# Background decoding of weights redistributed: six late pieces for twelve, w_sg between the halves of w_in, copies issued by ScalarE, later row stores

## The chip, the cores and the metric

The kernel runs on one core of one Trainium2 chip. The metric is the device time in microseconds (us), the median of three runs of the same program. Profiles come from one further execution, of which the hardware profiler recorded every instruction.

## The reference, cut to what matters

Three layers follow each other on a batch of 4 sequences of 576 rows; everything is float32 on entry to the matmuls, and the weights come as float64.

```
ret  = ((q @ k.T) / 8 * Dmat) @ v          # 8 heads of 64, Dmat = gamma_h ** (i - j) for i >= j, else 0
x    = ret, heads joined                   # 4 x 576 x 512
h    = gelu(x @ w_in);  u, v = h[:512], h[512:]
v_n  = (v - mean(v)) / sqrt(var(v) + 1e-6) * g_ln
v_s  = w_sg @ v_n + b_sg                   # w_sg is 576 x 576: it mixes rows of a sequence
x    = x + (u * v_s) @ w_out               # token mixer
xn   = (x - mean(x)) / sqrt(var(x) + 1e-6) * g_ln2
out  = x + relu(xn @ w_ch1) @ w_ch2        # channel mixer, 512 -> 2048 -> 512
```

## The kernel before

Every product is taken with float32 accuracy from three faster ones: an operand is split into a high part (`hi`, a rounded copy by ScalarE) and a low part (`lo`, the difference, by POOL or VectorE), and `mm3` multiplies hi with hi, hi with lo, lo with hi (lines 124 to 126).

**Stages, in order of time.** (1) The attention, 16 units (4 sequences by 4 pairs of heads), up to 82 us. A unit's inputs are one load `ld` (line 203; four buffers, issued three units ahead by SP, the queue of SyncE), prepared by ScalarE (`prep_unit`, line 218); its states are copied by ScalarE (`y`, line 252) and then decayed by VectorE (line 254). (2) The token mixer, batch by batch, 82 to 309 us: `v_tile` makes the five v tiles (`split_x`'s `xt_hi`, `xt_lo` by w_in's second half), whose rows are normalised (`bn_stats` at line 476 up to line 492) and split into `vnh`, `vnl`; `u_chunk` makes u; `sg_chunk` multiplies `vnh`, `vnl` by w_sg, adds b_sg (`b_bc`), multiplies u (lines 597, 600) and splits the result into `glh`, `gll` (lines 608 to 611); `w_out_tile` multiplies by w_out (line 661) and stores rows of x. In the batches' course `turn_x` transposes rows of the attention's result (line 632) and stores them to DRAM, from where they come back for the residual. The fifth v tile has 64 rows only; its rows are copied to the place where the next batch needs them by three DMAs (lines 550, 551). (3) The channel mixer, 309 us to the end: three blocks of rows by eight steps, 24 steps s in all; each step forms the products of one group of channel weights by seven products instead of eight, with VectorE instructions named `h`, `t`, `u` and `b` at lines 929 to 956, and 26 matmul triples with line 124 among them. The block's rows come as eight loads of features `x_raw` (line 764), scaled, combined by POOL (line 786) and split into `fe`.

**Background.** Weights are float64 in DRAM. A piece of 128 x 512 is loaded as words (`raw`, line 134, three buffers), decoded by four VectorE instructions (lines 142, 146, 149, 151) with one Square by ScalarE (line 148) before the last, and then either split into hi and lo (w_in, w_out) or stored back to DRAM as float32 (`w1_dram`, `w2_dram`, line 360, for the 32 pieces of the channel mixer). Decoded words `c` have two buffers. w_sg is float32: its five row groups (`raw_sg`, line 321, sharing the three `raw` buffers) are only split. All this is one generator, `background_steps`, and `background(n)` takes n steps of it; a step is one VectorE instruction of a piece, or one row group of w_sg. The calls stand in the code of the stages: twice one step a unit in the attention, and in the mixer after each v tile, u chunk, gate chunk and w_out tile as the table `PACE` says (a row per batch; the last row is for quarter steps of the channel mixer). `LATE` is the number of the 32 channel pieces that are left to the channel mixer. A new piece is loaded when one is taken up, so that one or two loads are ahead.

**Order.** The schedule is manual: every engine works through its instructions in the order in which the code issues them, SP's DMAs too. `after(n, f)` puts work off by n ticks; a tick follows each gelu and most other parts, and work that is due then is issued in turn, an instruction of each.

## Time and profile before

| | us |
|---|---|
| runs | 732.44, 731.85, 732.58; median 732.44 |
| profiled execution, device time | 730.41 |
| its span in the trace | 728.5 |
| attention | 0 to 82 |
| token mixer, batches 1 to 4 | 82 to 147.7, 206.0, 257.5, 309.2 |
| channel mixer, step 0, 1, 5, 7, 9, 15 begins | 309.2, 316.6, 401.8, 438.0, 474.3, 568.7 |

The span is the stretch between the first and the last instruction recorded; the device time has 1.9 us around it. TensorE's two clock levels here are 1.2 and 2.4 GHz, and a granted clock of 1.00 in a row means the higher one. The ends of the stages are the starts of the next stage's first matmul on TensorE; VectorE may still be at work for the stage before.

### The profile page before, as it was taken

The page shows a single profiled execution, that of the slowest core. Times are in us where ns is not written, and L with a number is a line of the kernel's source. Part 1 is how long each engine was busy: PE and PEld are TensorE (multiplying, and loading weights), DVE is VectorE, ACT ScalarE, POOL GpSimd, SP SyncE. Part 2 cuts the span into 40 slices and gives each one's busy share as a digit, 9 for nine tenths or more (in the row PEclk, how much of TensorE's full clock was granted, in tenths as well). Part 3 has the DMA queues.
Part 4 walks back from the last instruction along what each step waited for, and adds up shares of the span by engine and source line. Part 5 has one row for each costly group of instructions (what it writes and reads, how often), then busy time and mean ns, then how long its engine had stood idle before and what let it go on. Part 6 is the DMA issues. An engine that isn't in the chain of part 4 may idle for free.

```text
span 728.5 us, 11598 instructions
## 1 busy us (share of the span) xinstructions
PE 679.0 (93%) x4294; PEld 600.0 (82%) x4294; DVE 502.9 (69%) x929; ACT 289.3 (40%) x529; POOL 335.1 (46%) x302
## 2 busy tenths in 40 slices
PE   6989988899999998869878998999999899999997
PEld 4878887699899898667767787898988788989895
DVE  2889849799798879877887866566755655344333
ACT  2434445345346364423334444334434443333321
POOL 0321265725426435834443367555455845544511
PEclk9999998999999999889999999999999999999999
DMA  9998253485675694465574621453642144212132
GB/s 349 340 330 328 67 156 98 144 269 159 208 240 162 189 251 132 143 242 159 181 219 135 173 87 58 158 176 116 188 114 90 58 145 145 72 59 73 57 116 86
DMA packets 61960, 117.88 MB, mean 162 GB/s; under 512 B 6480, under 2 KB 25424, under 8 KB 59984
## 3 DMA queue, kind: packets, MB, share of 16 engines
q1 hardware_dynamic: 61904, 117.15, 50.5%
q8 instruction: 33, 0.54, 0.3%
q14 instruction: 23, 0.19, 0.1%
HBM read 89.07 MB, written 27.26 MB: 160 GB/s over the span
## 4 chain that ended last, share of the span: by engine, by line
PE 53%; DVE 17%; DMA 10%; POOL 7%; ACT 6%; issue 4%; SPq 2%; DVEq 0%; POOLq 0%; ACTq 0%
PE b L124 14%; PE b L126 14%; PE b L125 14%; PE b L661 7%; DMA ld<-in_attn_dram 4%; POOL mix L786 2%; DVE c L151 2%; DVE c L146 2%; DVE c L142 2%; SPq L764 1%; DVE h L929 1%; DMA raw_w<-w_dram 1%; DMA w_dram<-c 1%; PE o L285 1%; ACT h L928 1%
## 5 line engine op out<-in xcount | busy, mean ns | idle before, releaser
L124 PE MATMUL b<-fe,w 128*128 128x384 f32 x336 | 118.2, 352 | 22.4 <-DVE t L951 9.1
L729 POOL TENSOR_TENSOR w<-raw_w,w 128x512 fp32r<-128x512 f32 x46 | 61.9, 1346 | 127.3 <-ACT w L728 127.3
L125 PE MATMUL b<-fe,w 128*128 128x384 f32 x336 | 115.8, 345 | 0.0
L126 PE MATMUL b<-fe,w 128*128 128x384 f32 x336 | 115.8, 345 | 0.0
L126 PE MATMUL b<-w,h 128*128 128x512 f32 x288 | 114.7, 398 | 0.0
L124 PE MATMUL b<-w,h 128*128 128x512 f32 x288 | 114.5, 398 | 0.0
L125 PE MATMUL b<-w,h 128*128 128x512 f32 x288 | 114.2, 396 | 0.0
L928 ACT ACTIVATE h<-b 128x384 fp32r<-128x384 f32 x72 | 35.3, 491 | 151.0 <-DVE b L956 111.5
L124 PEld LDWEIGHTS b<-fe,w 128*128 128x128 f32 x336 | 64.7, 193 | 33.8 <-DVE t L951 12.6
L929 DVE SCALAR_TENSOR_TENSOR h<-b,h 128x384 fp32r<-128x384 f32 x72 | 40.1, 556 | 46.3 <-ACT h L928 46.3
L715 POOL TENSOR_TENSOR w<-raw_w,w 128x768 fp32r<-128x768 f32 x23 | 43.4, 1887 | 57.8 <-ACT w L714 51.7
L125 PEld LDWEIGHTS b<-fe,w 128*128 128x128 f32 x336 | 65.1, 194 | 3.4
L148 ACT ACTIVATE raw<-raw 128x512 f32<-128x512 f32 x44 | 30.1, 685 | 93.7 <-DVE c L146 73.0
L126 PEld LDWEIGHTS b<-w,h 128*128 128x128 f32 x288 | 54.5, 189 | 13.2
L126 PEld LDWEIGHTS b<-fe,w 128*128 128x128 f32 x336 | 65.0, 194 | 0.0
L125 PEld LDWEIGHTS b<-w,h 128*128 128x128 f32 x288 | 54.7, 190 | 9.5
L124 PEld LDWEIGHTS b<-w,h 128*128 128x128 f32 x288 | 54.8, 190 | 8.9
L956 DVE TENSOR_TENSOR b<-b,u 128x384 f32<-128x384 f32 x48 | 26.9, 560 | 38.1 <-PE b L126 38.0
L481 POOL TENSOR_TENSOR st<-st,par 128x1 f32<-128x1 f32 x36 | 24.1, 679 | 62.7 <-DVE st L480 53.9
L714 ACT CAST w<-raw_w 128x1024 fp32r<-128x1024 f32 (+1 forms) x47 | 44.2, 942 | 12.8 <-POOL w L729 7.0
L715 DVE TENSOR_TENSOR w<-raw_w,w 128x1024 fp32r<-128x1024 f32 x24 | 34.6, 1441 | 14.4 <-ACT w L714 14.4
L373 POOL TENSOR_TENSOR xt_lo<-xb,xt_hi 128x576 fp32r<-128x576 f32 x16 | 25.0, 1573 | 41.4 <-ACT xt_hi L372 32.7
(133 smaller groups left out, 1611.6 us busy)
## 6 DMA issues: line engine op xcount, KB each, us to landing
ld<-in_attn_dram SPq DMA_DIRECT2D x15, 1120.0 KB, 7.6
raw<-in_w_ch_dram SPq DMA_DIRECT2D x32, 512.0 KB, 4.7
raw_w<-w_dram SPq DMA_DIRECT2D x24, 512.0 KB, 4.6
raw_w<-w_dram SPq DMA_DIRECT2D x46, 256.0 KB, 2.6
w_dram<-c SPq DMA_DIRECT2D x32, 256.0 KB, 2.6
row<-y_dram SPq DMA_DIRECT2D x30, 256.0 KB, 4.7
x_r<-x_dram SPq DMA_DIRECT2D x18, 256.0 KB, 4.9
y_dram<-x_r SPq DMA_DIRECT2D x18, 256.0 KB, 2.1
```

The lines of the kernel that those rows point to most:

```text
L124: pe.matmul(ps, lh, rh, start=first, stop=False, skip_group_check=True)
L125: pe.matmul(ps, lh, rl, start=False, stop=False, skip_group_check=True)
L126: pe.matmul(ps, ll, rh, start=False, stop=last, skip_group_check=True)
L148: act.activation(out=f(w1), in_=f(w1), func=ACTF.Square)
L373: pool.tensor_tensor(out=lo[:, k, 0:S], in0=xb[b][:, k], in1=f(hi[:, k, 0:S]), op=ALU.subtract)
L661: pe.matmul(ps, g, wo[k][:, w], start=done[0] == 1, stop=done[0] == 3 * KE, skip_group_check=True)
L714: act.copy(hi, r)
L715: (pool if s and part else dve).tensor_tensor(out=lo, in0=r, in1=f(hi), op=ALU.subtract)
L729: pool.tensor_tensor(out=t[:, 1], in0=raw, in1=f(t[:, 0]), op=ALU.subtract)
L928: act.activation(out=t[:, 0], in_=v, func=ACTF.Relu)
L929: dve.scalar_tensor_tensor(out=t[:, 1], in0=v, scalar=0.0, in1=f(t[:, 0]), op0=ALU.max, op1=ALU.subtract)
L956: dve.tensor_tensor(out=v, in0=v, in1=u, op=ALU.add)
```

## The change

The number of late pieces goes from 12 to 6, so that six more pieces are decoded before the channel mixer; the channel mixer begins its background work with the second step (q > 3, four quarters to a step). `PACE` has new numbers. w_in's decoding is cut into its second half, which comes first as before, and its first half, and w_sg's loads and splits come between the two instead of behind both. In the attention the first call in odd units takes two steps. The three copies of the fifth v tile's rows are issued by ScalarE's queue. The stores of x's transposed rows are issued two ticks after the transpose.

```diff
-    ("13233", "3432", "2220", "34333"),
...
-    "2222",
+    ("11211", "3432", "2220", "34333"),
...
+    "1112",
-LATE = 12
+LATE = 6
...
-    def load_w_in():
-
-        wi.extend(slot("w_in").rearrange("p (a n) -> p a n", a=2) for k in range(KE))
-        for x in (512, 0):
-            c = slice(x, x + 512)
-            for k in range(KE):
-                yield (w_in[k, :, c], wi[k][:, 0, c], wi[k][:, 1, c])
+    def load_w_in(x):
+        c = slice(x, x + 512)
+        for k in range(KE):
+            if x:
+                wi.append(slot("w_in").rearrange("p (a n) -> p a n", a=2))
+            yield (w_in[k, :, c], wi[k][:, 0, c], wi[k][:, 1, c])
...
-        yield from f64_pieces(load_w_in(), 1)
+
+        yield from f64_pieces(load_w_in(512), 1)
         yield from load_w_sg()
+        yield from f64_pieces(load_w_in(0))
...
-            background(1)
+            background(2 if n % 2 else 1)
...
-                        nc.sync.dma_start(out=r[h * R:(h + 1) * R], in_=t[R:])
-                    nc.sync.dma_start(out=t[R:], in_=t[0:R])
+                        act.dma_start(out=r[h * R:(h + 1) * R], in_=t[R:])
+                    act.dma_start(out=t[R:], in_=t[0:R])
...
-        for q in range(4):
-            nc.sync.dma_start(
...
+        def store():
+            for q in range(4):
+                nc.sync.dma_start(
...
+        after(2, store)
...
-        background(int(PACE[B][q % 4]) if blk == 0 else 0)
+        background(int(PACE[B][q % 4]) if blk == 0 and q > 3 else 0)
```

The first place is ScalarE in the attention, at units 10 to 12; before, its queue reads as follows. `y_684` is the copy of unit 10, `ld_656` the input of unit 12, and `c` is a decoded piece of w_in.

```order
L218 ACTIVATE ld_596<-ld_596,tab3_98 128x4x64 x2
L148 ACTIVATE raw_500<-raw_500 128x512
L252 COPY y_684<-us_94 128x64
L218 ACTIVATE ld_656<-ld_656,tab0_95 128x4x64 x2
L252 COPY y_739<-us_94 128x64
L294 CAST w_in_155<-c_612 128x512
L218 ACTIVATE ld_709<-ld_709,tab1_96 128x4x64 x2
L148 ACTIVATE raw_610<-raw_610 128x512
L252 COPY y_794<-us_94 128x64
```

Now it reads so; `y_698` is unit 10, `ld_664` the input of unit 12, and `raw_sg` are row groups of w_sg.

```order
L218 ACTIVATE ld_603<-ld_603,tab3_98 128x4x64 x2
L294 CAST w_sg_657<-raw_sg_660 128x576
L294 CAST w_sg_657<-raw_sg_678 128x576
L252 COPY y_698<-us_94 128x64
L294 CAST w_sg_658<-raw_sg_682 128x576
L218 ACTIVATE ld_664<-ld_664,tab0_95 128x4x64 x2
L294 CAST w_sg_659<-raw_sg_722 128x576
L252 COPY y_756<-us_94 128x64
L327 CAST w_sg_659<-raw_sg_740 128x576
```

Four casts of w_sg have come in; two of them stand between the preparation for unit 11 and the copy of unit 10.

The second place is VectorE at unit 12, before: `y_794` is that unit's, `raw_610` a piece of w_in that was taken up a unit earlier.

```order
L146 SCALAR_TENSOR_TENSOR c_725<-raw_610,c_725 128x512
L231 TENSOR_TENSOR p_770<-sc_91,tab0_95 128x1024
L149 SCALAR_TENSOR_TENSOR c_725<-raw_610,c_725 128x512
L254 SCALAR_TENSOR_TENSOR y_794<-y_794,tab0_95,us_94 128x64 x3
L259 TENSOR_TENSOR pr_799<-us_94,tab0_95 128x64
L288 TENSOR_TENSOR xb_649<-o1_93,tab3_98 128x576
L151 SCALAR_TENSOR_TENSOR c_725<-raw_610,c_725 128x512
```

Now `y_816` is unit 12's, and `raw_796` the first piece of w_in's first half.

```order
L231 TENSOR_TENSOR p_786<-sc_91,tab0_95 128x1024
L142 TENSOR_SCALAR c_802<-raw_796 128x512
L254 SCALAR_TENSOR_TENSOR y_816<-y_816,tab0_95,us_94 128x64 x3
L259 TENSOR_TENSOR pr_821<-us_94,tab0_95 128x64
L288 TENSOR_TENSOR xb_653<-o1_93,tab3_98 128x576
L146 SCALAR_TENSOR_TENSOR c_802<-raw_796,c_802 128x512
```

The first instruction on a new piece has come directly ahead of unit 12's `y`.

SP's loads around that place are now these, `ld_782` being unit 14's input; before, w_sg's loads came only behind the attention.

```order
L320 DMA raw_sg_722<-in_w_sg_dram 128x576
L203 DMA ld_726<-in_attn_dram 128x2240
L320 DMA raw_sg_740<-in_w_sg_dram 128x576
L203 DMA ld_782<-in_attn_dram 128x2240
L134 DMA raw_796<-in_w_in_dram 128x1024
L134 DMA raw_798<-in_w_in_dram 128x1024
L134 DMA raw_800<-in_w_in_dram 128x1024
L203 DMA ld_841<-in_attn_dram 128x2240
```

The piece `raw_796` is issued directly behind unit 14's load, and three pieces precede unit 15's load.

The third place is the fourth batch of the token mixer. On SP, before, the features' loads (two rows of four) have one store of a decoded piece behind them and none between.

```order
L360 DMA w1_dram_99<-c_2814 128x512
L134 DMA raw_2852<-in_w_ch_dram 128x1024
L764 DMA x_raw_2856<-z_dram_70 32x12x128 x4
L764 DMA x_raw_2857<-z_dram_70 32x12x128 x4
L360 DMA w2_dram_100<-c_2854 128x512
L134 DMA raw_2929<-in_w_ch_dram 128x1024
L639 DMA x_dram_69<-x_t_2934 32x4x128 x4
L360 DMA w2_dram_100<-c_2931 128x512
```

Now another store of a piece follows them, and two pieces' loads and stores more.

```order
L359 DMA w2_dram_100<-c_2859 128x512
L134 DMA raw_2883<-in_w_ch_dram 128x1024
L684 DMA y_dram_71<-x_r_2841 128x512
L771 DMA x_raw_2904<-z_dram_70 32x12x128 x4
L771 DMA x_raw_2905<-z_dram_70 32x12x128 x4
L359 DMA w2_dram_100<-c_2885 128x512
L134 DMA raw_2930<-in_w_ch_dram 128x1024
L359 DMA w1_dram_99<-c_2932 128x512
L134 DMA raw_2959<-in_w_ch_dram 128x1024
L359 DMA w1_dram_99<-c_2961 128x512
```

VectorE's queue there, before, has the statistics of two tiles (lines 476 to 492, `bs` and `st`) ahead of the next piece.

```order
L149 SCALAR_TENSOR_TENSOR c_2854<-raw_2634,c_2854 128x512
L151 SCALAR_TENSOR_TENSOR c_2854<-raw_2634,c_2854 128x512
L476 BN_STATS bs_2919<-t_2893 128x6
L478 BN_AGGR st_2920<-bs_2919 128x2
L480 TENSOR_SCALAR st_2920<-st_2920 128x1
L492 TENSOR_SCALAR st_2896<-st_2896 128x1
L142 TENSOR_SCALAR c_2931<-raw_2812 128x512
```

Now a whole piece more and the head of the next, `c_2961`, stand ahead of the statistics of tile `t_2946`.

```order
L142 TENSOR_SCALAR c_2932<-raw_2857 128x512
L477 BN_STATS bs_2948<-t_2926 128x6
L479 BN_AGGR st_2949<-bs_2948 128x2
L481 TENSOR_SCALAR st_2949<-st_2949 128x1
L146 SCALAR_TENSOR_TENSOR c_2932<-raw_2857,c_2932 128x512
L149 SCALAR_TENSOR_TENSOR c_2932<-raw_2857,c_2932 128x512
L151 SCALAR_TENSOR_TENSOR c_2932<-raw_2857,c_2932 128x512
L142 TENSOR_SCALAR c_2961<-raw_2883 128x512
L146 SCALAR_TENSOR_TENSOR c_2961<-raw_2883,c_2961 128x512
L477 BN_STATS bs_2978<-t_2946 128x6
```

`c_2961` takes the buffer of `c_2885`, whose store is the one behind the features' loads on SP.

## Rows read from the trace of the kernel before

**Rows 1.** The page's first part: busy us, share of the span, instructions.

```profile
PE 679.0 (93%) x4294; PEld 600.0 (82%) x4294; DVE 502.9 (69%) x929; ACT 289.3 (40%) x529; POOL 335.1 (46%) x302
```

**Rows 2.** Windows: length, busy PE, PEld, DVE, ACT, POOL, clock, DMA, GB/s.

```profile
82.00:147.69 65.69, 57.75 (x324) 51.54 (x321) 49.30 (x96) 30.10 (x57) 38.39 (x34) 0.92 0.43 128
147.69:206.00 58.31, 58.31 (x345) 53.02 (x344) 51.47 (x111) 24.22 (x47) 23.49 (x23) 1.00 0.69 219
206.00:257.50 51.50, 51.29 (x313) 47.01 (x312) 45.18 (x116) 24.19 (x45) 25.39 (x26) 1.00 0.64 193
257.50:309.24 51.74, 47.70 (x282) 42.87 (x281) 45.09 (x71) 26.54 (x49) 31.84 (x27) 0.93 0.63 170
316.55:401.76 85.21, 69.48 (x313) 58.68 (x313) 67.35 (x126) 32.09 (x54) 35.40 (x35) 0.94 0.56 173
```

**Rows 3.** Windows of line 124 alone: length, busy PE and PEld, clock, DMA, GB/s.

```profile
316.55:438.03 121.48, 60.40 (x156) 30.71 (x157) 0.94 0.53 160
474.26:568.71 94.45, 56.88 (x156) 29.30 (x156) 1.00 0.44 130
```

**Rows 4.** Timeline of TensorE: start, us, instruction, in brackets the idle time before.

```profile
109.12 0.40 PE L124 MATMUL b<-w_sg,vnh 128*128 128x288 f32 x1 [2.22 <-ACT vnh L525]
...
293.37 1.65 PE L661 MATMUL b<-w_out,glh 128*128 128x512 f32 x3 [1.99 <-ACT glh L608]
...
326.52 0.69 PE L124 MATMUL b<-fe,w 128*128 128x384 f32 x1 [5.62 <-DVE u L949]
```

**Rows 5.** Timeline of VectorE in the first batch of the mixer.

```profile
105.20 0.43 DVE L142 TENSOR_SCALAR c<-raw 128x512 uint32<-128x512 uint32 x1 [6.41 <-DMA raw<-in_w_out_dram]
```

**Rows 6.** Timeline of SP in the same stretch: start, us, the DMAs issued.

```profile
79.92 14.42 SPq L321 DMA_DIRECT2D raw_sg<-in_w_sg_dram  x5
...
97.93 1.18 SPq L550 DMA_DIRECT2D v_rest<-t  x2
...
101.44 1.50 SPq L134 DMA_DIRECT2D raw<-in_w_out_dram  x3
```

**Rows 7.** Windows of the tile c alone: length, busy DVE, ACT, POOL.

```profile
147.69:206.00 58.31, 27.45 (x38) 0.00 (x0) 0.00 (x0) 1.00 0.69 219
316.55:401.76 85.21, 28.02 (x36) 0.00 (x0) 0.00 (x0) 0.94 0.56 173
```

**Rows 8.** DMA issues from 0 to 100 us: KB each, median us to landing.

```profile
raw<-in_w_in_dram SPq DMA_DIRECT2D x8, 512.0 KB, 7.9
...
raw_sg<-in_w_sg_dram SPq DMA_DIRECT2D x5, 288.0 KB, 2.9
...
v_rest<-t SPq DMA_DIRECT2D x2, 128.0 KB, 2.3
```

**Rows 9.** The chain that ended last, from 45 to 62: start, us, what.

```profile
50.94 9.29 DMA ld<-in_attn_dram
```

**Rows 10.** Timeline of SP in the attention.

```profile
60.37 0.33 SPq L203 DMA_DIRECT2D ld<-in_attn_dram  x1
```

**Rows 11.** Timeline of VectorE in the attention.

```profile
56.35 0.90 DVE L254 SCALAR_TENSOR_TENSOR y<-y,tab,us 128x64 f32<-128x64 f32 x3
...
65.43 0.59 DVE L254 SCALAR_TENSOR_TENSOR y<-y,tab,us 128x64 f32<-128x64 f32 x2
```

**Rows 12.** The tile x_raw, 250 to 290: duration in ns, first and last start.

```profile
L764 SPq DMA_DIRECT2D x_raw<-z_dram x8: 452/687/3056, 257.4 to 264.4; - x8
```

**Rows 13.** The chain that ended last, in the fourth batch of the mixer.

```profile
265.38 6.56 DMA w_dram<-c
```

**Rows 14.** Timeline of VectorE in the fourth batch.

```profile
261.26 0.42 DVE L142 TENSOR_SCALAR c<-raw 128x512 uint32<-128x512 uint32 x1
...
272.04 1.07 DVE L142 TENSOR_SCALAR c<-raw 128x512 uint32<-128x512 uint32 x1 [1.56 <-DMA w_dram<-c]
273.14 2.22 DVE L146 SCALAR_TENSOR_TENSOR c<-raw,c 128x512 uint32<-128x512 uint32 x1
...
285.32 0.49 DVE L597 SCALAR_TENSOR_TENSOR b<-b,par,b_bc 128x288 f32<-128x288 f32 x1
```

**Rows 15.** Timeline of POOL in the same stretch.

```profile
272.90 4.18 POOL L786 TENSOR_TENSOR x_raw<-x_raw 128x768 f32<-128x768 f32 x2
```

More of the change, by code (lines that the diff above doesn't have):

```diff
@@ L40 @@
 PACE = (
-    ("13233", "3432", "2220", "34333"),
-    ("04122", "2322", "1110", "23321"),
-    ("01012", "1130", "1200", "22220"),
-    ("01220", "2031", "0000", "00220"),
-    "2222",
+    ("11211", "3432", "2220", "34333"),
+    ("05132", "2433", "2131", "34332"),
+    ("01012", "2240", "2401", "33322"),
+    ("12545", "3051", "0301", "00220"),
+    "1112",
 )
-LATE = 12
+LATE = 6
 HIDDEN = {
@@ L637, in turn_x @@
         to = x_dram[y_rows.index((b if i < NC else b | 1, i)), at:at + n]
-        for q in range(4):
-            nc.sync.dma_start(
-                out=to[:, q * 128:(q + 1) * 128].rearrange("(a j) c -> j a c", j=32),
-                in_=t[q * 32:(q + 1) * 32].rearrange("j (a c) -> j a c", c=128),
-            )
+        def store():
+            for q in range(4):
+                nc.sync.dma_start(
+                    out=to[:, q * 128:(q + 1) * 128].rearrange("(a j) c -> j a c", j=32),
+                    in_=t[q * 32:(q + 1) * 32].rearrange("j (a c) -> j a c", c=128),
+                )
+            yield
+        after(2, store)
     def load_x(b, i):
```

## The prediction

> **What bounds the kernel now.** I read the busy line first: TensorE works 93% of the span [rows 1], so a change pays only where TensorE stands still or is granted less clock. Then the windows by stage. TensorE is busy for 57.75 of 65.69 us in the first batch's mixer, for all 58.31 and 51.29 of 51.50 in the second and third, and for 47.70 of 51.74 in the fourth [rows 2]. VectorE (DVE), in the second and third batch, is already at 88%.
>
> The largest loss is in the channel mixer, which is one loop over 24 steps s. Two windows of six steps each hold the same 156 matmuls of line 124: steps 1 to 6 take 121.48 us, steps 9 to 14 take 94.45 [rows 3]. The first six differ by the decoding of late weight pieces on VectorE; they lose 121.48 - 94.45 = 27.0 us. (Steps 7 and 15 take 20.10 and 19.50, decoding or not; what they lose is the next block's features, and stays.) Third, the timeline of TensorE with the idle time before an instruction [rows 4]: 2.22 us for `vnh` at 109.12, 1.99 for `glh` at 293.37, 5.62 for VectorE's `u` at 326.52.
>
> Why the first mixer waits stands in the queues. At 105.20 VectorE has stood for 6.41 us at an instruction that needs a piece of w_out [rows 5]; behind it are the statistics of v's tiles, which `vnh` needs. That piece was issued by SyncE (SP) only at 101.44, behind v's copies at 97.93, and these behind five loads of w_sg that began at 79.92 [rows 6].
>
> **The change, part by part.** The sum is made against the profiled execution, 730.4 us, which is 2.0 below the median of the three runs, 732.4.
>
> *Late pieces.* Each of the 32 channel-weight pieces is four VectorE instructions. Twelve late ones were 48, at two per quarter step from the loop's start; six are 24, five per step, in steps 1 to 5 only. 40 of the 48 stood in steps 1 to 6 (two pieces in step 0). In proportion, 24/40 of the loss stays, 16.2 us, and 10.8 are won; at most all 27.0 are. I take the upper part, because the loss is not in proportion: VectorE did 67.35 us of work in steps 1 to 4, 28.02 of it in 36 decoding instructions [rows 2, 7], 0.78 each, so it has (67.35 - 28.02) / 4 = 9.8 us a step of its own. With nine decoding instructions a step it came to 16.8, over the 94.45 / 6 = 15.7 us that TensorE needs; with five it comes to 13.7, under it. I leave 1 us a step for instructions that stand in front of an `h` or `u`, 7 in all: **-20**.
>
> *w_sg between w_in's halves.* w_sg and the later half of w_in are now begun in the attention. What this removes: w_sg's splits from the stretch after 82 us, and with them the 6.41 us wait, since w_out's pieces are issued right behind `b_bc` and long landed when VectorE gets there. VectorE's order behind that point is unchanged in the first batch, so everything that it gates moves up by 6.4 us at least; TensorE idles for 65.69 - 57.75 = 7.9 there, and a granted clock of 0.92 means some (1 - 0.92) x 65.69 = 5 more lost at 1.2 GHz in place of 2.4 [rows 2], in stretches that begin behind such stalls; about half of that I count as won back at most. New is that w_in's last piece is split only beside the last v tile, some 0.7 us late for u's first chunk, and that ScalarE now waits for v's first two copies, 2.3 us from issue to landing [rows 8], before it issues the third; behind it stand two gelus and two tiles' `vnh`, needed 8 us later, which covers it. I take **-9** (-6.4 to -11). The same wait in the third batch I take as covered too (0 to +2).
>
> What it adds in the attention: (a) at unit 10 ScalarE's queue has the cast of w_sg's second row ahead of the copy of `y`, and SP issues that row's load directly behind unit 12's, which in this trace was issued at 50.94 and took 9.29 us [rows 9]. So the row lands past 60.2, its cast ends near 61.5, and unit 10's `y`, at 56.35 in this trace [rows 11], starts 4.5 to 5.5 us later. (b) At unit 12 VectorE's queue has the first decode of w_in's later half (its columns 0 to 511) ahead of `y`, and its piece is issued in the step before, behind unit 14's load. That load was issued at 60.37 [rows 10] and will be some 4.5 later; a piece takes 7.9 us from issue to landing in this stage [rows 8], so it lands near 72 and `y`, at 65.43 before [rows 11], starts near 72. What (a) cost is inside this, because the transfers catch up during the wait. The attention ends about **+6.5** later (+4 to +8.5; the low end if the queue has drained and the piece takes nearer the 2.9 of a w_sg row [rows 8]).
>
> *Decoding moved into the mixers.* Counted in VectorE's order, the second batch gets 42 for 30, the third 29 for 20, the fourth 18 that do work for 15. An instruction of the four costs 27.45 / 38 = 0.72 us there [rows 7]. Second batch: 51.47 + 12 x 0.72 = 60.1 in 58.31, 2 over. Third: 45.18 + 9 x 0.72 = 51.7 in 51.50, under 1 over. Bounds: 0, if the overhang falls where TensorE has banks in hand, and +6, if it all falls on `glh`. I take **+2.5**.
>
> The trace shows such an instruction at a mean of 0.72 us, and at 2.22 at 273.14, beside POOL's L786 [rows 7, 14, 15]. The Trainium skill (SBUF — State Buffer, Who interferes with whom) says that a VectorE instruction with two SBUF inputs and a GpSimd instruction that reads SBUF exclude each other for the whole instruction. By that rule alone, with each of the 21 moved ones meeting POOL, they would cost 21 x (2.22 - 0.72) = 31 us more and the kernel would be slower, near 750. The mean of 0.72, in a stretch where POOL works 23.49 of 58.31 us [rows 2], says that most meet nothing; I give it 2 in 100, inside the slower side below.
>
> *The fourth batch.* Decoded words `c` have two buffers. The store behind SP's eight loads of features (257.4 to 264.4 [rows 12]) was issued at 265.38 and took 6.56, and VectorE stood until 272.04 for it [rows 13, 14]. It hit the second piece after, when v's statistics were done. Now four decodes more precede: the piece that needs that buffer stands in front of the statistics of the last two v tiles. VectorE will arrive near 261, where it begins the last piece that need not wait now [rows 14], and stand to 272 or, as the third batch makes the loads later, 275. Behind the landing then stand 12 decodes x 0.72 = 8.6, two tiles' statistics at 1.7, four transposes at 0.7 and some trips to ScalarE of 1 us each, near 21 us; in this trace 285.32 - 272.04 = 13.3 passed from there to the first eviction of the gate [rows 14]. I take **+8** for `gll`, which gates w_out's products (0 if the store gets ahead of the loads, +12 with half clock behind the longer stall).
>
> *Stores of x's rows.* They leave SP's path by two ticks; SP's waits there covered nothing that TensorE waits for in batches two to four: 0 to -2, taken as 0.
>
> Sum: -20 - 9 + 6.5 + 2.5 + 8 = **-12**. 730.4 - 12 = 718.4 for a profiled execution, 732.4 - 12 = **720** for the median.
>
> **Rivals.** (A) *The new waits cost little.* The late pieces give 22, the first mixer 10, and the attention 2 only, with nothing in batches two to four: -30, 702. For it: the attention has idle TensorE time already, and a landing there can be 3 us. Against it: both waits stand in an order that nothing between can overtake. (B) *Slower: the late loss is one of position.* If TensorE loses time in every step in which any decode stands between `u`, `t` and `h` on VectorE, five of six steps keep their 4.5 us and only 27.0 / 6 = 4.5 are won. Then -4.5 - 9 + 6.5 + 2.5 + 8 = +3.5, 736. It decides once less than 8 of the 27 come back. For it: the waits [rows 4] name VectorE's short instructions, not a full queue. Against it: VectorE has instructions between `h` and `u` in steps 9 to 14 too, and they lose nothing [rows 3]. (C) *The moves cancel:* within 0.2%, 731 to 734; the sum would have to be some 12 too good, for instance if the late pieces give 8 only. That the change doesn't do what it says I exclude: the order shows each move.
>
> **Chances.** Forecast (710 to 728) 55%, A 22%, B with the contention above 18%, C 5%. A measurement here tells 0.2%, 1.5 us, from no change. Faster by more: 55 + 22 = 77%; same 5%; slower 18%. The range holds 8 in 10: from 702, inside A, to 734, which leaves out half of B's weight and the lower part of A's.
>
> **What would show it.** Right: steps 1 to 6 take near 101 us for 121; no idle time of 6 us ahead of w_out's first decode; unit 10's `y` waiting for ScalarE, and a decode waiting for w_in's piece ahead of unit 12's; the attention's end 6 to 7 us later and the first batch's end 2 to 3 us earlier than now; in the fourth batch a VectorE wait of 10 us for `w_dram<-c`, and TensorE waiting for `vnh` ahead of the gate. Wrong: steps 1 to 6 above 113 us, which is B; or the attention's end within 2 us of now and no long wait for the store, which is A.

## The result, and the profile after

The changed kernel takes 736.29 us (median of 6 runs, 734.01 to 736.72), the kernel before 732.14 beside it (728.39 to 732.66): a ratio of 1.0062, 95% interval 1.0038 to 1.0086. It is 0.6% slower, where 720 was forecast and the range ended at 734. The time is that of rival B (736), but by luck, not by B's mechanism: the late pieces gave more than forecast, and the stages ahead of them lost it again and more. The profiled execution spans 734.5 us (728.5 before), 6.0 more.

The stages, each from the start of its first large group of products on TensorE's timeline to the next one's, in us; "forecast" is the term of the sum:

| stage | before | after | difference | forecast |
|---|---|---|---|---|
| attention | 82.22 | 96.27 | +14.05 | +6.5 |
| first batch | 65.47 | 59.97 | -5.5 | -9 |
| second batch | 52.07 | 54.73 | +2.7 | +2.5, with the third |
| third batch | 52.54 | 63.43 | +10.9 | (above) |
| fourth batch | 56.94 | 64.75 | +7.8 | +8 |
| channel mixer, steps 1 to 6 | 121.48 | 98.22 | -23.3 | -20 |
| step 0 and steps 7 to 23 | 297.78 | 297.16 | -0.6 | 0 |

In this table the third and the fourth batch begin with their first products, for the kernel before at 199.76 and 252.30. The 206.0 and 257.5 of the table of times and of [rows 2] lie some 6 and 5 us behind these. The prediction's two sums come out nearly the same with the windows below: VectorE 45.44 + 8.6 = 54.1 us in 52.07, and 46.07 + 6.5 = 52.6 in 52.54.

The windows of the four batches, first of before and then of after (the columns are those of [rows 2]):

```profile
82.22:147.69 65.47, 57.53 (x320) 51.39 (x317) 49.30 (x96) 29.89 (x56) 38.39 (x34) 0.92 0.43 127
147.69:199.76 52.07, 52.07 (x317) 47.84 (x316) 45.44 (x98) 22.25 (x44) 22.34 (x22) 1.00 0.68 211
199.76:252.30 52.54, 52.33 (x317) 47.88 (x316) 46.07 (x121) 24.59 (x46) 25.24 (x27) 1.00 0.63 196
252.30:309.24 56.94, 52.90 (x305) 47.19 (x304) 50.22 (x79) 28.11 (x52) 33.14 (x28) 0.94 0.65 179
```

```profile
96.27:156.23 59.96, 54.94 (x320) 48.99 (x317) 46.94 (x97) 27.05 (x52) 31.61 (x29) 0.97 0.38 110
156.23:210.96 54.73, 53.25 (x318) 47.64 (x316) 51.69 (x101) 22.66 (x45) 23.85 (x22) 1.00 0.71 231
210.96:274.39 63.43, 56.02 (x318) 50.54 (x317) 50.26 (x132) 25.73 (x48) 24.84 (x27) 0.92 0.59 186
274.39:339.13 64.74, 54.93 (x305) 49.02 (x304) 50.31 (x87) 29.42 (x55) 35.16 (x28) 0.87 0.63 181
346.44:444.66 98.22, 96.36 (x470) 84.35 (x469) 75.89 (x136) 44.36 (x77) 54.48 (x49) 1.00 0.49 153
```

The last row is steps 1 to 6 of the channel mixer, which answer to the first of [rows 3]: TensorE is now busy for 96.36 of 98.22 us at full clock. The batches tell where it went: the third and the fourth hold the same products as before, but TensorE stands for 63.43 - 56.02 = 7.4 and 64.74 - 54.93 = 9.8 us, and the granted clock has fallen to 0.92 and 0.87. The contention with POOL, to which the prediction gave 2 in 100, did not come: the 42 decoding instructions in the window of the second batch take 30.70 us, 0.73 each, and the 33 of before took 24.22, the same 0.73.

**Attention.** VectorE's timeline after, where unit 10's `y` and unit 12's stand (56.35 and 65.43 in [rows 11]):

```profile
63.05 0.91 DVE L254 SCALAR_TENSOR_TENSOR y<-y,tab,us 128x64 f32<-128x64 f32 x3 [4.99 <-ACT y L252]
...
76.98 0.43 DVE L142 TENSOR_SCALAR c<-raw 128x512 uint32<-128x512 uint32 x1 [5.32 <-DMA raw<-in_w_in_dram]
77.32 0.91 DVE L254 SCALAR_TENSOR_TENSOR y<-y,tab,us 128x64 f32<-128x64 f32 x3
```

ScalarE's timeline, behind the first wait:

```profile
62.24 0.67 ACT L294 CAST w_sg<-raw_sg 128x576 fp32r<-128x576 f32 x1 [3.75 <-DMA raw_sg<-in_w_sg_dram]
62.82 0.20 ACT L252 COPY y<-us 128x64 f32<-128x64 f32 x1
```

SP's timeline ahead of the second:

```profile
69.33 0.33 SPq L203 DMA_DIRECT2D ld<-in_attn_dram  x1
69.75 2.60 SPq L134 DMA_DIRECT2D raw<-in_w_in_dram  x3
```

Both waits of the forecast are there, at the named places. But unit 14's load goes out at 69.33, 9.0 later than in [rows 10] and not 4.5, and the piece behind it at 69.75. The load takes the buffer that unit 10 gives back. Unit 10's `y` begins 6.7 us later than before, by the wait of 4.99 and by 1.7 that the attention was behind already. Between the wait and the load the last products of unit 10 and the first of unit 11 ran at a granted clock of 0.51, where they had 1.00 before. That took 2.2 us more (windows, before first):

```profile
57.44:60.37 2.93, 2.85 (x56) 2.51 (x57) 2.68 (x4) 0.11 (x1) 0.00 (x0) 1.00 0.83 297
64.16:69.30 5.14, 5.14 (x58) 4.57 (x58) 2.71 (x6) 2.56 (x6) 3.77 (x4) 0.51 0.44 160
```

**Third batch.** ScalarE's timeline after, with the three copies in its queue (ACTq):

```profile
227.13 1.12 ACTq L551 DMA_DIRECT2D v_rest<-t  x2
232.56 0.47 ACTq L552 DMA_DIRECT2D t<-t  x1
233.08 0.41 ACT L501 ACTIVATE u<-b 128x288 f32<-128x288 f32 x1 [5.98 <-DMA v_rest<-t]
```

TensorE's timeline there, which had no wait of over 0.3 us in this gate before:

```profile
238.21 0.40 PE L124 MATMUL b<-w_sg,vnh 128*128 128x288 f32 x1 [1.55 <-ACT vnh L526]
...
243.43 0.61 PE L124 MATMUL b<-w_sg,vnh 128*128 128x288 f32 x1 [3.47 <-ACT vnh L526]
```

The third copy must wait for the first two, ScalarE works in order, and a gelu and the last tiles' `vnh` stand behind it. The first two took 4.9 us (the DMA view after; the same copies on SP, in this batch before, are in the second fence):

```profile
v_rest<-t ACTq DMA_DIRECT2D x2, 128.0 KB, 4.9
```

```profile
v_rest<-t SPq DMA_DIRECT2D x2, 128.0 KB, 2.3
```

ScalarE's queue by itself does not make them longer: in the first batch of the changed kernel, where SP has no load under way, the same two copies on it take 2.4 us.

```profile
v_rest<-t ACTq DMA_DIRECT2D x2, 128.0 KB, 2.4
```

What differs in the third batch stands in SP's timeline. After, SP goes past them and issues a piece and a row just ahead of them:

```profile
224.65 0.38 SPq L134 DMA_DIRECT2D raw<-in_w_ch_dram  x1
225.08 0.45 SPq L745 DMA_DIRECT2D rows<-y_dram  x1
```

Before, the piece came behind the copies in SP's order:

```profile
212.30 1.11 SPq L550 DMA_DIRECT2D v_rest<-t  x2
215.19 0.46 SPq L551 DMA_DIRECT2D t<-t  x1
215.71 0.58 SPq L134 DMA_DIRECT2D raw<-in_w_ch_dram  x1
```

**Fourth batch.** VectorE's wait for the store behind the features' loads, 1.56 in [rows 14]:

```profile
294.27 0.43 DVE L142 TENSOR_SCALAR c<-raw 128x512 uint32<-128x512 uint32 x1 [7.54 <-DMA w_dram<-c]
```

TensorE's timeline behind it:

```profile
303.73 0.61 PE L124 MATMUL b<-w_sg,vnh 128*128 128x288 f32 x1 [3.38 <-ACT vnh L526]
...
307.97 0.61 PE L124 MATMUL b<-w_sg,vnh 128*128 128x288 f32 x1 [2.23 <-ACT vnh L526]
```

**First batch.** The 6.41 us wait of [rows 5] is gone, and with it the 2.22 us for `vnh` of [rows 4]. TensorE now waits 3.77 us for the next batch's `xt_lo` (its timeline), and the granted clock of the stage is 0.97. With the copies issued by SP (the first experiment) that wait is 2.2 us and the clock 1.00.

```profile
143.36 0.50 PE L126 MATMUL b<-w_in,xt_lo 128*128 128x512 f32 x1 [3.77 <-POOL xt_lo L372]
```

### The profile page after: what moved, and what is told of

Read it like the earlier page. It is cut to its first block, busy times and chain, and to the rows that moved or that the text cites. A ratio compares the mean times of both kernels' runs of the same rounds, so it can differ in the third digit from the quotient of the medians.

```text
span 734.5 us, 11605 instructions
## 1 busy us (share of the span) xinstructions
PE 679.8 (93%) x4294; PEld 599.8 (82%) x4294; DVE 496.2 (68%) x929; ACT 289.3 (39%) x529; POOL 338.7 (46%) x302
## 4 chain that ended last, share of the span: by engine, by line
PE 42%; DVE 8%; POOL 5%; issue 3%; ACT 3%; DMA 1%; SPq 1%; POOLq 0%; DVEq 0%; ACTq 0%
PE b L124 13%; PE b L126 13%; PE b L125 13%; POOL mix L793 3%; PE b L668 2%; ACT h L935 1%; DVE h L936 1%; DMA w_dram<-c 1%; POOL w L736 1%; DVE fe L801 1%; DVE b L963 1%; SPq L771 1%; DVE row L986 1%; DVE t L958 1%; DVE c L146 1%
## 5 line engine op out<-in xcount | busy, mean ns | idle before, releaser
L124 PE MATMUL b<-fe,w 128*128 128x384 f32 x336 | 114.8, 342 | 8.4 <-DVE t L958 5.7
L125 PE MATMUL b<-fe,w 128*128 128x384 f32 x336 | 113.3, 337 | 0.0
L126 PE MATMUL b<-fe,w 128*128 128x384 f32 x336 | 113.1, 337 | 0.0
L124 PEld LDWEIGHTS b<-fe,w 128*128 128x128 f32 x336 | 63.0, 188 | 17.2 <-DVE t L958 7.9
L125 PEld LDWEIGHTS b<-fe,w 128*128 128x128 f32 x336 | 63.1, 188 | 3.5
L126 PEld LDWEIGHTS b<-w,h 128*128 128x128 f32 x288 | 54.1, 188 | 13.0
L126 PEld LDWEIGHTS b<-fe,w 128*128 128x128 f32 x336 | 63.1, 188 | 0.0
L125 PEld LDWEIGHTS b<-w,h 128*128 128x128 f32 x288 | 54.1, 188 | 9.5
L124 PEld LDWEIGHTS b<-w,h 128*128 128x128 f32 x288 | 54.0, 188 | 8.7
L124 PE MATMUL b<-w_sg,vnh 128*128 128x288 f32 x128 | 41.0, 320 | 12.9 <-ACT vnh L526 11.8
L721 ACT CAST w<-raw_w 128x1024 fp32r<-128x1024 f32 (+1 forms) x47 | 44.2, 943 | 13.5 <-POOL raw_w L712 7.9
L527 POOL TENSOR_TENSOR vnl<-t,vnh 128x512 fp32r<-128x512 f32 x18 | 25.4, 1413 | 45.2 <-ACT vnh L526 45.2
```

The costliest lines, as they stand in the source:

```text
L124: pe.matmul(ps, lh, rh, start=first, stop=False, skip_group_check=True)
L125: pe.matmul(ps, lh, rl, start=False, stop=False, skip_group_check=True)
L126: pe.matmul(ps, ll, rh, start=False, stop=last, skip_group_check=True)
L527: pool.tensor_tensor(out=vl[:, i], in0=t, in1=f(vh[:, i]), op=ALU.subtract)
L721: act.copy(hi, r)
```

## The experiments

Stage lengths as in the table above, each from one profiled execution; the ratio is to the kernel before, run on the same chip, whose median was 730.0 to 732.6. "Undone" is the changed kernel with w_sg's order and SP's copies put back.

The old order of w_sg has a side effect that the expectations do not name. Each call of `f64_pieces` begins with a background step that loads and decodes nothing. The changed kernel takes w_in's pieces in two such calls, the old order in one. So in the runs with the old order every later decoding instruction stands one step earlier: in VectorE's order 85 stand ahead of the second batch's gate for 84, and in the fourth batch 17 are left for 18. The run with old steps in attention has one step fewer besides, and with it the places of the changed kernel from the second batch on.

| run | median us | ratio (95%) | attention | batches 1 to 4 | steps 1 to 6 |
|---|---|---|---|---|---|
| changed | 736.29 | 1.0062 (1.0038 to 1.0086) | 96.27 | 59.97, 54.73, 63.43, 64.75 | 98.22 |
| changed, copies by SP | 729.39 | 0.9965 (0.9939 to 0.9992) | 97.06 | 56.01, 54.70, 60.02, 64.90 | 98.07 |
| before, copies by ScalarE | 737.34 | 1.0078 (1.0050 to 1.0106) | 84.39 | 67.11, 52.07, 56.38, 56.15 | 121.51 |
| changed, old order of w_sg | 722.78 | 0.9874 (0.9847 to 0.9901) | 86.45 | 60.53, 56.62, 60.09, 61.55 | 98.12 |
| changed, 8 late, old 4th table | 737.57 | 1.0081 (1.0053 to 1.0108) | 96.16 | 60.67, 54.69, 63.67, 54.25 | 110.73 |
| undone | 715.91 | 0.9781 (0.9732 to 0.9830) | 86.05 | 55.28, 57.27, 58.03, 61.70 | 98.07 |
| undone, stores at once | 716.28 | 0.9780 (0.9738 to 0.9822) | 84.33 | 56.90, 57.39, 58.32, 61.94 | 98.07 |
| undone, 9 late, old 3rd and 4th tables | 722.26 | 0.9853 (0.9806 to 0.9900) | 86.43 | 55.30, 56.81, 57.49, 54.39 | 109.39 |
| undone, 9 late, old 2nd table | 727.15 | 0.9931 (0.9908 to 0.9953) | 86.59 | 55.33, 53.11, 56.41, 63.55 | 113.27 |
| undone, old steps in attention | 728.88 | 0.9951 (0.9930 to 0.9971) | 86.15 | 64.38, 54.77, 59.83, 64.56 | 98.09 |
| changed, w_sg row earlier | 733.99 | 1.0023 (0.9999 to 1.0048) | 91.35 | 59.81, 54.87, 63.23, 65.47 | 98.10 |
| the same, w_in piece earlier too | 729.72 | 0.9963 (0.9944 to 0.9982) | 86.01 | 60.55, 54.88, 63.48, 67.37 | 98.26 |
| undone, old 4th table | 714.70 | 0.9799 (0.9758 to 0.9839) | 84.72 | 55.29, 57.05, 57.58, 60.79 | 98.11 |

**The copies by SP again.**

```diff
-act.dma_start(out=r[h * R:(h + 1) * R], in_=t[R:])
+nc.sync.dma_start(out=r[h * R:(h + 1) * R], in_=t[R:])
...
-act.dma_start(out=t[R:], in_=t[0:R])
+nc.sync.dma_start(out=t[R:], in_=t[0:R])
```

> The changed kernel with v's three copies issued by SP again, nothing else. Theory: in the third batch of the mixer (210.96 to 274.39, 63.4 us in the changed kernel, 52.5 before) the 10.9 us are lost because ScalarE stands 5.98 us at the third copy, so that vnh is late and TensorE falls to the lower clock. Then this batch takes 53 to 56 us, the other stages stay within 1 us, and the kernel is 7 to 10 us faster than the changed one, 726 to 729. Rival 1: the third batch loses by its nine further decoding instructions on VectorE; then it stays at 61 or more and the time at 734 to 737. Rival 2: SP is now the later queue, the copies wait behind loads there, and half of it comes back, 731.

The kernel gained 6.9 us, just under the 7 to 10 expected, with 3.4 in the third batch and 4.0 in the first, where the forecast had the wait covered. So the copies are only a third of the third batch's 10.9; at 60.02 that batch lies between the theory and rival 1. Rival 2's time, 731, is not far, but its reason falls: on SP the copies land in 2.3 us in both batches that have them.

**The copies by ScalarE, alone**, in the kernel before (the diff the other way round).

> The kernel before with v's three copies issued by ScalarE, nothing else. Theory: the wait of ScalarE for its first two copies is the cost by itself wherever vnh is near; in the third batch the copies are issued at 212 and land in 2.3 us here, so the wait is 2 to 3 us there and the kernel is 1 to 5 us slower than before, 733 to 737; the first batch is covered. Rival (the wait costs only together with the fuller queues of the changed kernel): within 1 us of before.

5.5 us slower, just over the 1 to 5 expected: 3.8 in the third batch and 1.6 in the first, which was not covered. (The attention's 2.2, with the same order of instructions there, are looked at below.) ScalarE stands nearly as long as in the changed kernel:

```profile
216.09 1.12 ACTq L550 DMA_DIRECT2D v_rest<-t  x2
221.07 0.47 ACTq L551 DMA_DIRECT2D t<-t  x1
221.59 0.41 ACT L500 ACTIVATE u<-b 128x288 f32<-128x288 f32 x1 [5.53 <-DMA v_rest<-t]
```

The copies are a cost by themselves, and the rival, that they need the changed kernel's fuller queues, falls. Here too SP's loads go out beside them, and the two copies take 4.5 us.

**The old order of w_sg.**

```diff
-yield from f64_pieces(load_w_in(512), 1)
-yield from load_w_sg()
-yield from f64_pieces(load_w_in(0))
+yield from f64_pieces((p for x in (512, 0) for p in load_w_in(x)), 1)
+yield from load_w_sg()
```

> The changed kernel with w_sg behind the whole of w_in again, as before; seven more background steps in the attention stay, and everything else. Theory: the attention's 14.05 us are two waits that follow each other, unit 10's y for the cast of a w_sg row that lands late, and unit 12's y for a piece issued behind unit 14's load. With the old order both are gone, and the first product of the mixer is at 77 to 79 (91.12 in the changed kernel, 77.07 before); the first batch is longer by 1 to 5 us than the 59.96 of the changed kernel; the kernel is 8 to 12 us faster than the changed one, 724 to 728. Rival 1: the seven further steps themselves cost the attention its time; it ends at 85 or later and the kernel stays above 731. Rival 2: the 6.4 us wait for w_out comes back whole with a lower clock, 730 to 733.

13.5 us faster than the changed kernel, more than the 8 to 12 expected. The attention ends 9.8 earlier, and the first batch costs little more than with w_sg ahead (60.53 against 59.97): what made the first batch shorter was not the place of w_sg but the seven further steps in the attention. The run "undone, old steps in attention" below shows that from the other side. The third and the fourth batch are 3.3 and 3.2 shorter and the second 1.9 longer. That is the earlier step, not w_sg: "undone, old steps in attention" has the old order without the earlier step, and its batches 2 to 4 (54.77, 59.83, 64.56) are those of the changed kernel with copies by SP (54.70, 60.02, 64.90).

**Which waits in the attention.** First w_sg's second row one step earlier (two rows loaded at the first step), then also w_in's piece two steps ahead of its first decode, and one piece ahead instead of two:

```diff
-            if k < NC:
...
+            for j in islice(rows_in, 2 if k < 0 else 1):
...
-        yield from f64_pieces(load_w_in(0))
+        later = f64_pieces(load_w_in(0), 1)
+        yield next(later)
+        yield
+        yield
+        yield from later
```

> The changed kernel with w_sg's second row loaded one background step earlier (two rows ahead instead of one), nothing else. Theory: unit 10's y waits 4.99 us for a cast whose row is issued behind unit 12's load; with the row issued ahead of that load the wait is under 1 us, and the attention ends 4 to 7 us earlier (first product of the mixer at 89 to 92 instead of 96.27, counted from the large group of products); the wait at unit 12 for w_in's piece stays at 4 to 6 us. The kernel is 4 to 7 us faster than the changed one. Rival: the transfers of the attention are the bound (1.4 MB of w_sg more in it); the wait moves to the next unit's load and the end stays at 94 or later.

> The changed kernel with w_sg's second row one step earlier, and besides the first piece of w_in's later half loaded two background steps ahead of its first decoding instruction, one piece ahead instead of two; the two steps are made up for in the last two units. Theory: the wait of 5.47 us at unit 12 is the time from issue to landing of that piece; with two steps between it is under 1.5 us, and the attention ends at 85 to 88 (91.35 with the early row alone, 96.27 in the changed kernel). The kernel is 3 to 6 us faster than with the early row alone, 728 to 731. Rival: the transfers are the bound; the end stays at 90 or later.

The end moves from 96.27 to 91.35 and to 86.01, 4.9 and 5.3 us. Not all of the first is the edit's: these executions differ before they reach the edited place. The table has the start of each unit's last group of products (line 285) on TensorE's timeline:

| | unit 9 | unit 10 | unit 11 | unit 12 | end of the attention |
|---|---|---|---|---|---|
| before | 55.28 | 59.31 | 64.27 | 68.40 | 82.22 |
| changed | 58.20 | 67.53 | 72.18 | 81.05 | 96.27 |
| w_sg row earlier | 56.20 | 60.08 | 68.23 | 76.17 | 91.35 |
| w_in piece earlier too | 57.03 | 60.91 | 67.06 | 72.14 | 86.01 |
| undone | 57.35 | 62.55 | 66.79 | 71.61 | 86.05 |

From unit 9 on the changed kernel takes 38.1 us, the two runs 35.2 and 29.0: 2.9 for the first edit and 6.2 for the second. The medians say the same in kind, 2.3 and 4.3 us faster, so the first run missed its 4 to 7. The reason stands in VectorE's timeline of the first run. Unit 10's wait is nearly gone, but unit 11's `y` now waits 4.02 us for the cast of the next row of w_sg, and the second wait is still whole, only earlier:

```profile
56.88 0.91 DVE L254 SCALAR_TENSOR_TENSOR y<-y,tab,us 128x64 f32<-128x64 f32 x3 [0.81 <-ACT y L252]
...
63.75 0.91 DVE L254 SCALAR_TENSOR_TENSOR y<-y,tab,us 128x64 f32<-128x64 f32 x3 [4.02 <-ACT y L252]
...
72.07 0.43 DVE L142 TENSOR_SCALAR c<-raw 128x512 uint32<-128x512 uint32 x1 [5.47 <-DMA raw<-in_w_in_dram]
```

So no run takes away the first wait alone. That the two add up shows in the changed kernel itself: from unit 9 to 10 it takes 9.33 us for 4.03 before, from unit 11 to 12 8.87 for 4.13, and in between only 0.3 is won back. The rival, that the transfers bind, falls: the last run moves the same bytes.

What the place of w_sg costs is then about 10 us: from unit 9 on the three runs with the changed kernel's attention take 36.6 to 39.9 us, the six with the old order and all seven steps 27.8 to 28.7. The other 4 of the 14.05 can't be put down to the change. Three executions with the old attention (before, copies alone, old steps) end it at 82.22, 84.39 and 86.15, and the profiled execution of before was the earliest.

**The fourth batch and eight late pieces.**

```diff
-    ("12545", "3051", "0301", "00220"),
-    "1112",
+    ("01220", "2031", "0000", "00220"),
+    "2222",
-LATE = 6
+LATE = 8
```

> The changed kernel with eight late pieces for six, two per quarter step (eight per step, in steps 1 to 4), and the table of the fourth batch as before, so that no further piece stands ahead of the statistics there. Theory for the fourth batch (64.7 us in the changed kernel, 56.9 before): its loss is VectorE's wait of 7.54 us for the store behind the features' loads; without it 57 to 59. Theory for the late pieces: the loss is what VectorE has over TensorE's 15.7 us a step; eight a step come to 9.8 + 8 x 0.78 = 16.0, and steps 1 to 6 take 99 to 102 us (98.2 with five a step). Together 3 to 6 us faster than the changed kernel, 730 to 733. Rival (late loss in proportion to the instructions, 27.0 for 40): 32 lose 21.6, the steps take 116, and the kernel is 10 slower, 746.

The fourth batch fell by 10.5 us to 54.25, as the theory has it and more, and VectorE's wait for the store from 7.54 to 1.5. The late steps missed it: 110.73, between the 99 to 102 expected and the rival's 116, and the kernel with them (737.57 for 730 to 733). VectorE's busy time in steps 1 to 4, in which 28 of the 32 instructions run, shows that it was not full:

```profile
336.75:413.94 77.19, 68.10 (x313) 58.99 (x313) 58.55 (x116) 30.69 (x52) 35.12 (x35) 0.96 0.55 166
```

58.55 us of work, or 61.7 with the other four instructions, are less than the 4 x 15.7 = 62.9 that TensorE needs for these steps, so it is not that VectorE has too much. TensorE's waits in the six steps are for VectorE's `h`, `u` and `t` (3.7, 3.7 and 3.2 us), which fits rival B's reason, the place of the decoding ahead of them; no run moves the same number to other places within a step. At eight a step it costs 4 us a step, at five a step 98.22 - 94.45 = 3.8 us in all.

**Both undone; stores at once.** The diffs of the copies and of the order together, and then besides `for _ in store(): pass` in place of `after(2, store)`:

> The changed kernel with both undone: w_sg behind the whole of w_in as before, and v's copies issued by SP as before. Theory: the two costs are in different stages and add up; the old order alone is at 722.8, the copies by SP alone gained 6.6 us (4.0 in the first batch, 3.4 in the third). Then 715 to 718. Rival: the copies' cost came from what the attention had delayed, and the old order has it already; 721 to 723.

> The kernel with both undone, and the stores of x's transposed rows issued at once again, as before. My prediction priced the later stores at nothing: then within 1.5 us of the kernel with both undone. Rival 1: the later stores keep SP free for loads that VectorE waits for, and undoing them costs 2 us or more. Rival 2: they put stores ahead of the x rows' loads later on, and undoing them gains 2 or more.

The gains add up, 6.9 and 13.5 to 20.4: 715.91, 2.2% faster than the kernel before (1.7 to 2.7) and 2.8% faster than the changed one. Issuing the stores at once moves nothing that can be told, which is the prediction's zero.

**Where the decoding belongs.** Both undone, nine late pieces from step 0 on, and the old tables of the third and fourth batch:

```diff
-    ("01012", "2240", "2401", "33322"),
-    ("12545", "3051", "0301", "00220"),
-    "1112",
+    ("01012", "1130", "1200", "22220"),
+    ("01220", "2031", "0000", "00220"),
+    "1212",
...
-LATE = 6
+LATE = 9
...
-        background(int(PACE[B][q % 4]) if blk == 0 and q > 3 else 0)
+        background(int(PACE[B][q % 4]) if blk == 0 else 0)
```

> The kernel with both undone, and nine late pieces for six: the tables of the third and the fourth batch as in the kernel before, and six decoding instructions per step of the channel mixer from step 0 on, 36 in all. Theory: decoding ahead of the statistics delays vnh and lowers TensorE's clock, 7.5 us in the third batch and 8 in the fourth; both come back (third 52 to 54, fourth 55 to 58). The late steps: the runs so far lose 3.8 us with 24 instructions, 16.3 with 32 at eight a step, 27.0 with 48 at eight; six a step in steps 0 to 5 I put at 8 to 12. Net 4 to 9 us faster than with both undone. Rival (it is the number of late instructions that counts, not the number per step): the late steps lose 20 and the kernel is 1 to 4 us slower.

The fourth batch came back (54.39), the third hardly (57.49), and the late steps lost 109.39 - 94.45 = 14.9 with 36 instructions at six a step, over the 8 to 12 expected. Net 6 slower, where 4 to 9 faster was expected: the rival's sign, by a mean of 11.3 / 12 = 0.9 us for each further late instruction.

The same nine late pieces, with the old table of the second batch in place of the third's and fourth's:

```diff
-    ("05132", "2433", "2131", "34332"),
+    ("04122", "2322", "1110", "23321"),
```

> The kernel with both undone, the table of the second batch as in the kernel before (12 background steps fewer there), nine late pieces at six instructions a step from step 0. Theory: with nine late pieces and old tables for the third and fourth batch the third still took 57.5 us for 52.5, so its loss comes from the second: VectorE enters the third batch 2 us late by the second's twelve further decodes, vnh is late, and TensorE runs part of the gate at 1.2 GHz. Then the second batch takes 52 to 53 (57.3 with both undone) and the third 52 to 55 (58.0), the fourth stays at 61 to 62, the late steps take 109. Net 715 to 719. Rival: the third batch's loss is from its own nine decodes after all and the other run hid it; it stays at 57 or more, the kernel at 720 or more.

The second batch is at 53.11 as expected, the third at 56.41, 1.6 better for twelve steps fewer ahead of it. It ends between theory and rival: 3.9 us over before remain. The kernel, 727.15, is 8 us over the 715 to 719 expected, since the late steps took 113.27, with the same table that took 109.39 in the run above; why they differ stays open.

Both undone, with six late pieces, and the old division of the steps between attention and first batch:

```diff
-    ("11211", "3432", "2220", "34333"),
+    ("13233", "3432", "2220", "34333"),
...
-            background(2 if n % 2 else 1)
+            background(1)
```

> The kernel with both undone, with one background step in odd units of the attention as before, and the first batch's table as before; the seven steps go back from the attention to the first batch. Theory: the attention's 84 to 86 us in the last three runs, 82.2 before, are the seven further steps and what they load; it ends 2 to 4 us earlier (82 to 84), and the first batch, 55.3, gets back part of the wait for w_out and takes 59 to 65. Net 3 to 7 us slower than with both undone, 719 to 723. Rival: the order of the copies' undoing alone made the first batch faster; then the first batch stays under 57 and the kernel is 2 us faster.

The first batch is 9.1 us longer with its old steps, and VectorE's wait for w_out is back in it (its waits, with total, times and longest):

```profile
DVE c L142 <- DMA raw<-in_w_out_dram: 6.9, 1, 6.9
```

The attention is the same to 0.1, so a cost of the seven steps there can't be told from the spread of single executions; the theory's first half falls, its second holds. The kernel is 13 us slower than with both undone, for 3 to 7 expected: the third and fourth batch lose 1.8 and 2.9 besides, and the second gains 2.5, all by the one step by which decoding is later there.

**The fourth batch, place or number.** Both undone and the fourth table of before (`"01220", "2031", "0000", "00220"`), with the same number of instructions as with both undone, which is seventeen by VectorE's order:

> The kernel with both undone, and the fourth batch's table as in the kernel before, with six late pieces: the same number of decoding instructions in the fourth batch as with both undone, but eight of them behind the statistics of the last v tiles instead of ahead. Theory: in the fourth batch it is the place that costs, since the wait for the store behind the features' loads stands ahead of the statistics; it takes 55 to 58 us (61.7 with both undone, 64.8 in the changed kernel) and the kernel 710 to 713. Rival 1: it is the number; all eighteen must be done before the gate's first eviction anyway, so the batch stays at 61 to 63 and the kernel at 715 to 718. Rival 2: the wait now delays the gate's evictions and it gets worse, 719.

60.79 for 61.70: rival 1, nearly. `vnh` is in time now, but the waits have moved to the gate's end. TensorE's waits there, with total, times and longest:

```profile
PE b L667 <- ACT glh L608: 7.4, 3, 4.2
```

VectorE's timeline, where its wait now is, behind the last statistics:

```profile
277.30 0.43 DVE L142 TENSOR_SCALAR c<-raw 128x512 uint32<-128x512 uint32 x1 [5.47 <-DMA x_dram<-x_t]
```

The median, 714.70 (712.57 to 719.24), can't be told from that with both undone. Over all runs the batch goes with the number of decoding instructions in it: 54.25 us with 10, 54.39 with 14, 56.15 and 56.94 with 15, 60.79 to 63.55 with 17, 64.56 to 67.37 with 18. VectorE's longest wait for a store goes the same way, 1.5 to 2.5 us with 10 to 15 (the changed kernel with 8 late, before, undone with 9 late) and 5.5 to 7.5 with 17 or 18 (old 4th table, undone, changed). Which of the two sets the length no run separates.

## Why the prediction was wrong

*Late pieces (-20):* the size was right, -23.3. The reason given, VectorE's load against TensorE's 15.7 us a step, is not what sets the loss: for eight a step the same reckoning gave 102 at most, and 110.73 came. That it hit the size at five a step was in part luck.

*w_sg between w_in's halves (-9):* the wait for w_out went, but not by the place of w_sg. It goes with the seven further steps in the attention, which this step of the prediction does not name: the old order has the gain as well, and with the old steps the wait is back. Without ScalarE's copies the gain is 9.5 (56.01), the size forecast.

*ScalarE's wait for the copies (0 in the first batch, 0 to +2 in the third):* a step that failed. "Which covers it" is wrong, and so is taking it over to the third batch: both rest on 2.3 us to landing, a row of the first batch. The copies cost 4.0 us in the first batch and 3.4 in the third. In the third they take 4.9 us to land, and what differs from the 2.3 and 2.4 elsewhere is that SP, no longer held by them, has put its loads ahead. The Trainium skill (DMA: Bandwidth & Descriptors, Issuing engines are not separate DMA queues) says that transfers started by different engines run on the same 16 DMA engines and interleave, and that a second issuer saves sequencer time alone. The trace agrees: 4.9 us on ScalarE's queue behind SP's loads, 2.4 on the same queue with none ahead, and besides it ScalarE's stand of 5.98.

*Attention (+6.5):* a step that failed. Both waits were foreseen, place and cause. "What (a) cost is inside this, because the transfers catch up during the wait" is the wrong sentence. Unit 14's load takes the buffer that unit 10 gives back, and SP issues in order; so the first wait moves that load, and the piece behind it, by 9.0 us, and the second wait is added. The place of w_sg costs about 10 us where 6.5 was forecast. The other 4 of the 14.05 go with the profiled execution of before, the earliest of all at unit 9.

*Second and third batch (+2.5 for the decoding):* a step that failed, and the largest. With the copies by SP they are 2.6 and 7.5 over before, 10.1 in all and beyond the bound of +6. The prediction set VectorE's busy time against the length of the batch. But VectorE is not full in the third batch of the changed kernel (50.26 of 63.43 us); TensorE stands for `vnh`, with the copies by SP still once for 3.5 us, and the granted clock falls to 0.94 there. That `vnh` is late because decoding stands ahead of its statistics is argued from VectorE's order. Of the third batch's 7.5 a part is explained: the one earlier step gives 2.0 (and takes 2.6 in the second), the batch's own further decodes 0.5, the second batch's 1.6. The other 3.4 stay open: old tables for the second and third batch together were not run.

*Fourth batch (+8):* right in size, +7.8, and the waits named are there. That the price comes from their place ahead of the statistics is not borne out: with decodes behind the statistics only 0.9 comes back, while fewer of them in the batch give 7.3 (14 for 17) and 10.5 (10 for 18).

*Stores (0):* right.

The sum, -12, missed the +6.0 of the profiled executions by 18: 7.5 in the attention (some 4 of them by the early execution), 7.4 by the copies, 7.6 by the decoding in the second and third batch, with 3 to 4 the other way in the late steps.

## What to carry to other kernels

Two waits in different queues add up when the second one's transfer is issued only after a buffer that the first one holds: follow the issue, not the landing. A DMA that must wait for another DMA belongs on a queue that computes nothing; a duration from issue to landing holds for the stage it was read in. When decoding is moved, ask per step how many instructions come to stand ahead of the engine's next customer; five a step were nearly free here (0.16 us each), six to eight cost 0.4 to 0.6 us each. And an edit that cuts a generator in two can add an empty step and shift all that comes later: here one step was worth 2 to 3 us, one way or the other, in each of three batches.

## What was not expected of the hardware

The same two copies of 128 KB took 2.3 to 2.4 us from issue to landing in one place, on either queue, and 4.9 in another, with loads of 256 and 512 KB issued 2 to 3 us ahead of them. And the attention ended between 82.22 and 86.15 us in executions whose attention has the same instructions in the same order (the kernel before, the one with the copies alone, and the one with the old steps); they differ by 1.5 us at the first unit's `y` and by 3.2 at unit 9.
